# Attention put two more positions ahead of the feed-forward in a fused attention and feed-forward kernel

## The chip, the core and the metric

The kernel runs on one core of one Trainium2 chip. The metric is the device time of one execution in microseconds (us), the median of several runs. The core has five engines, each with its own in-order stream of instructions: PE (TensorE, the matrix unit, whose weight loads are listed apart as PEld), DVE (VectorE), ACT (ScalarE), POOL (GpSimd) and SP (SyncE, which here only issues transfers). They meet through semaphores. An instruction that waits holds back everything behind it on its own engine.

## The reference

```
k_all = concatenate([k_g, k_l]); v_all = concatenate([v_g, v_l])
out_g = softmax(scale * q_g @ k_all.T) @ v_all                # 32 global rows
s_ll  = where(|i - j| <= 32, scale * q_l @ k_l.T, -1e9)       # 512 local rows, band of 32
s_lg  = scale * q_l @ k_g.T
out_l = softmax(concatenate([s_lg, s_ll])) @ v_all
x = concatenate([out_g, out_l]).transpose(0, 2, 1, 3).reshape(B * S, H * D)   # 8 * 544 rows of 512
h = x @ w_in                                                  # 512 -> 2048
g = maximum(h, 0) + log1p(exp(-|h|))                          # softplus
out = g @ w_out                                               # 2048 -> 512
```

There are 8 batches of 8 heads, 512 local and 32 global positions and heads 64 wide; everything is float32.

## The kernel before

**Two streams of work.** The attention is done by head pairs m = 0 to 31, four pairs to a batch. Pairs 0 to 3 (batch 0) are done by a start-up sequence. Each later pair has three parts p = 0, 1, 2. `scores(m, p)` multiplies queries and keys on PE into the PSUM tile `s_ps`; for pairs 8 and up DVE adds the mask while it copies the tile to SBUF (line 315) and takes maxima by blocks (line 316). After part 2 come `maxima` (DVE and POOL, lines 329 to 339) and `probs`: DVE spreads the maxima (`mb`, line 347), POOL subtracts them (lines 352 to 355), ACT takes the exponential (line 356). `values(m, p)` multiplies the probabilities by the values on PE into `v_ps`; ACT copies the result out (lines 369 and 373) and DVE adds the overlapping columns (lines 374 and 375) into `x`.

**From a head pair to an input of the feed-forward.** After `values(m, 2)` the sums of the exponentials go to DRAM and back as a small tile `sc` (`combine`, lines 382 and 386), DVE inverts them (`invert`, lines 391 and 392), they go out again and come back spread over 64 partitions as `rb` (lines 393 and 396), and DVE multiplies `x` by `rb` into `xa` (`normalise`, line 404). At the start of a batch of the feed-forward, `split_x` makes of every `xa` a rounded high part `xh` (line 451) and the remainder `xl` (line 452). ACT and POOL do it for the pairs 0 and 2 of the batch, DVE for 1 and 3. There is one `xh` and one `xl` for each place, so that the last product of the batch before must have read them.

**The feed-forward.** For batch b and hidden block f (16 of them), 12 matmuls make the tile `h` from `xh`, `xl` and the weights `wi`; ACT and DVE make the softplus `e` (DVE has line 543); ACT and POOL split it into `gh` and `gl`; 12 more matmuls add the block into four output tiles `o`. A product of the second half, half a block at a time, follows one or two blocks behind the first half. In batch 0, DVE, ACT and POOL also put the weights into their final form (lines 479 to 498). The last 32 global rows of all batches are done at the very end as a "batch 8".

**One PSUM tile for all of the attention.** `s_ps` (from pair 6 on) and `v_ps` are all the same buffer, tag `a`, with `bufs=1`. Each `s_ps` or `v_ps` must therefore be copied out by DVE or ACT before the next of either can be started on PE.

**What sets the order.** `pieces()` gives each piece of attention a position: `scores(m, p)` stands at 12m + 4p, `values(m, p)` 22 positions (LAG) behind that, `invert(m)` at `end(m) + 3` and `normalise(m)` at `end(m) + 6`, with

```
def end(m):
    return 12 * m + 8 + LAG
```

So a head pair takes 12 positions and a batch 48, and from pair 8 on, one slot every two positions holds a piece with matmuls, scores and values in turn. `moe_items()` lists the feed-forward as items with a size (half a block, 6 matmuls, has size 2). The last loop of the function emits the items one by one. After each it works out the position `at` that the attention should have reached, from the share of the batch's items done, and emits all pieces up to it. `first` is the position at which batch 1 of the feed-forward begins; before, it is 36 + 30 + 6 = 72, the position of `normalise(3 + 4b)` less 48b. In batch 0, `at` runs from START = 69 to `first + 48`. PE keeps the order in which its matmuls are emitted; on the other engines a scheduler orders the instructions by its own estimate of when each is ready.

Of the kernel before, what the change touches and what calls it, by code (L numbers as in the profile page):

```python
# [16 lines left out]
B, H, SL, SG, D = 8, 8, 512, 32, 64  # L17
# [14 lines left out]
MPE = 8  # L32
LAG = 22
STEP = 3
GW = 75
W_AHEAD = 9
W_PRE = 12
# [16 lines left out]
def moe_over_global_local_attention(  # L54
# [223 lines left out]
    def load_v(m):  # L278
        t = pl.tile([P, 2, 6, 66], F32, tag="v", name=f"v{m}", bufs=2)
        nc.gpsimd.memset(t[:, :, :, D:D + 1], 1.0)  # L280
        nc.sync.dma_start(out=t[:, :, :, 0:D], in_=v[m - M0].rearrange("p (h c d) -> p h c d", h=2, d=D))
        st["v", m] = t
# [37 lines left out]
    def grid(t, start, *dims):  # L320
        base = t[0:32, start:start + 1]
        return bass.AP(base.tensor, base.offset, [list(base.ap[0])] + [list(d) for d in dims])
# [3 lines left out]
    def maxima(m):  # L326
        mt = st.pop(("mt", m))
        for a in range(1, 4):
            nc.gpsimd.tensor_copy(mt[0:32, GW * a:GW * a + GW], mt[32 * a:32 * a + 32, 0:GW])
        e0 = 4 * GW  # L330
        for u, du, off in ((0, 1, -2), (3, 1, 3)):
            nc.vector.tensor_reduce(grid(mt, e0 + u, (7, 6), (du, 2)), grid(mt, 3 + u, (12, 6), (du, 2), (off, 2), (GW, 4)), axis=AX.XY, op=ALU.max)
        nc.vector.tensor_reduce(grid(mt, e0 + 2, (7, 6), (4, 2)), grid(mt, 3 + 2, (12, 6), (7, 2), (GW, 4)), axis=AX.X, op=ALU.max)
        g = e0 + 44
        nc.vector.tensor_reduce(grid(mt, g, (1, 2)), grid(mt, 3 + 5, (36, 2), (12, 3), (3, 2), (GW, 4)), axis=AX.XYZ, op=ALU.max)
        nc.vector.tensor_copy(grid(mt, e0 + 5, (21, 2), (7, 3)), mt[0:32, g:g + 2].unsqueeze(2).to_broadcast([32, 2, 3]))
# [52 lines left out]
    def invert(m):  # L389
        sc, rows = st.pop(("sc", m))  # L390
        after(nc.vector.tensor_scalar(sc, sc, 1e-9, None, op0=ALU.add), "scores")
        nc.vector.reciprocal(sc, sc)
        nc.sync.dma_start(out=rows, in_=sc)
        rb = pl.tile([64, 2, 608], F32, tag="rb", name=f"rb{m}", bufs=1)
        r = rec_dram[2 * m:2 * m + 2]
        nc.sync.dma_start(out=rb, in_=r.unsqueeze(0).to_broadcast([64, 2, 608]))
        st["rb", m] = rb

    def normalise(m):
        b, j = divmod(m, H // 2)  # L400
        x, rb = st.pop(("x", m)), st.pop(("rb", m))
        y = xa[b, j] = pl.tile([P, 608], F32, tag="xa", name=f"xa{b}_{j}", bufs=4)
        for h in range(2):
            after(nc.vector.tensor_tensor(y[64 * h:64 * h + 64], x[0:64, h], rb[:, h], op=ALU.mult), "scores")  # L404
        nc.sync.dma_start(out=xg_dram[j, :, SG * b:SG * b + SG], in_=y[:, 160:192])
        ready.add((b, j))

    def end(m):
        return 12 * m + 8 + LAG

    def pieces():
        def piece(*fs):
            def go():
                for f in fs:
                    f()
            return go
        ps = []
        for m in range(M0, M):
            for p in range(NPC):
                fs = [lambda m=m, p=p: scores(m, p)]  # L420
                if m + 1 < M:
                    fs.append(lambda m=m, p=p: load(m + 1, p))
                if p == 2:
                    fs.append(lambda m=m: maxima(m))
                    fs += [lambda m=m, q=q: probs(m, q) for q in range(NPC)]
                ps.append((12 * m + 4 * p, piece(*fs)))
                fs = [lambda m=m, p=p: values(m, p)]
                if p == 2:
                    fs.append(lambda m=m: combine(m))
                    if m + 2 < M:  # L430
                        fs.append(lambda m=m: load_v(m + 2))
                    ps.append((end(m) + STEP, lambda m=m: invert(m)))
                    ps.append((end(m) + 2 * STEP, lambda m=m: normalise(m)))
                ps.append((12 * m + 4 * p + LAG, piece(*fs)))
        ps.sort(key=lambda t: t[0])
        return ps
# [172 lines left out]
    def loads(upto):  # L609
        while wk[0] < min(upto, len(order_w)):  # L610
            if order_w[wk[0]]:
                load_w(*order_w[wk[0]])
            wk[0] += 1
# [13 lines left out]
    load_v(M0)  # L627
    load_v(M0 + 1)
    loads(W_PRE + 2)
    first = end(H // 2 - 1) + 2 * STEP  # L630
    pcs = pieces()
    local = (scores0, lambda m, a: invert0((m, a), 4), lambda m, a: diag0((m, a), 4), turn0, evict0, values0, split0)
    glob = (scores0g, lambda n: invert0(n, 1), lambda n: diag0(n, 1), turn0g, evict0g, values0g, split0g)
# [110 lines left out]
```

## Time and profile before

| what | value |
|---|---|
| median of 3 runs | 1099.55 us (1097.02, 1099.55 and one of 4822.36) |
| the profiled execution: its own time, and its span | 1099.49 us, 1097.4 us |
| PE busy | 1037.4 us, 95% |
| DVE, ACT, POOL busy | 599.2 us (55%), 549.8 us (50%), 466.7 us (43%) |
| mean granted clock of PE | 0.977 |
| PE in the first 225 us | 184.5 us busy |
| PE from 225 to 1025 us | 789.4 us busy of 800 |

The span runs from the first to the last instruction in the profile; 2.1 us of the execution's own time lie outside it. A row of the timeline gives start, duration, engine, line, operation, tiles with their shapes, and how many instructions were merged. In square brackets stands how long the engine was idle just before, and what ended that. "issue" there means that the profile shows no releaser. Names carry no numbers in the profile, so the batch of an instruction is told from its time: batches of the feed-forward begin on PE at about 92, 241, 364, 484, 603, 722, 841 and 952 us. Some matmul records can be missing.

### The profile page before, as it was taken

Reading aid. Unit: us, or ns where it says so; the run is one execution under the profiler, and the core shown is the slowest. Engines: PE = TensorE matmul, PEld = TensorE weight load, DVE = VectorE, ACT = ScalarE, POOL = GpSimd, SP = SyncE. Lnnn points to the kernel's source line nnn. Section 1 sums busy time; section 2 is a strip of 40 time slices with the busy share of each in tenths; the row PEclk is TensorE's granted clock in tenths of the full one; section 3 lists DMA queues with packets and bytes.
Section 4 is the critical chain, followed back from the end, with each engine's and each line's share of the span. In section 5 each row is a group of like instructions: output and inputs, shape, how many; then the busy total and the mean of one; then the engine's idle time right before and its main releaser. Section 6 shows DMA issues by size and latency. Waiting matters only on the chain.

```text
span 1097.4 us, 14272 instructions
## 1 busy us (share of the span) xinstructions
PE 1037.4 (95%) x5108; PEld 799.0 (73%) x5108; DVE 599.2 (55%) x1137; ACT 549.8 (50%) x972; POOL 466.7 (43%) x554
## 2 busy tenths in 40 slices
PE   6896788999999999999999999999999999999996
PEld 4674566767777777777777777777777778788895
DVE  5979697874445655565555544565546542311211
ACT  6855555544444544545444544554454544454452
POOL 2136475762345444454444344544445442222221
PEclk9997889999999999999999999999999999999998
DMA  9432332322112212123211312122212210110010
GB/s 359 157 98 86 108 129 64 94 53 84 50 49 49 89 44 55 47 54 93 55 48 52 93 44 55 48 81 53 55 45 55 84 28 13 32 39 1 1 39 20
DMA packets 78566, 74.14 MB, mean 68 GB/s; under 512 B 53380, under 2 KB 57476, under 8 KB 78496
## 3 DMA queue, kind: packets, MB, share of 16 engines
q1 hardware_dynamic: 77952, 73.17, 22.6%
q8 instruction: 40, 0.66, 0.2%
q14 instruction: 30, 0.25, 0.1%
q10 hardware_dynamic: 544, 0.07, 0.0%
HBM read 63.51 MB, written 9.71 MB: 67 GB/s over the span
## 4 chain that ended last, share of the span: by engine, by line
PE 74%; DVE 8%; DMA 4%; issue 3%; POOL 1%; ACT 1%; DVEq 0%; ACTq 0%; SPq 0%; POOLq 0%
PE h L124 30%; PE o L124 30%; PE v_ps L124 9%; PE s_ps L124 5%; DMA rb<-rec_scratch 3%; DVE xa L404 2%; DMA rec_scratch<-sc 1%; DVE xl L452 1%; DVE xh L451 1%; DVE s L315 1%; DVE mb L347 0%; DVE wbitswo L489 0%; DVE woraw L492 0%; DMA raw<-in_qk 0%; DVE wbitswo L486 0%
## 5 line engine op out<-in xcount | busy, mean ns | idle before, releaser
L124 PE MATMUL h<-xh,wi 128*128 128x512 f32 (+1 forms) x1152 | 357.9, 394 | 20.0 <-DVE xl L226 10.3
L124 PE MATMUL o<-wo,gh 128*128 128x512 f32 x1088 | 346.9, 400 | 0.0
L547 POOL TENSOR_TENSOR gl<-e,gh 128x512 fp32r<-128x512 f32 x136 | 178.5, 1313 | 378.9 <-ACT gh L546 322.7
L124 PEld LDWEIGHTS h<-xh,wi 128*128 128x128 f32 x1152 | 208.7, 190 | 69.7 <-issue 17.2
L124 PEld LDWEIGHTS o<-wo,gh 128*128 128x128 f32 x1088 | 201.4, 189 | 47.3 <-issue 4.0
L124 PE MATMUL h<-xl,wi 128*128 128x512 f32 (+1 forms) x576 | 221.1, 384 | 2.8 <-DVE xl L452 2.8
L540 ACT ACTIVATE e<-h 128x512 f32<-128x512 f32 x136 | 81.3, 598 | 272.3 <-PE h L124 265.5
L124 PE MATMUL o<-wo,gl 128*128 128x512 f32 x544 | 213.6, 393 | 0.0
L543 DVE SCALAR_TENSOR_TENSOR e<-h,e 128x512 f32<-128x512 f32 x136 | 93.2, 685 | 182.9 <-ACT e L542 182.9
L352 POOL TENSOR_TENSOR s<-s,mb 128x384 f32<-128x384 f32 x112 | 137.7, 1261 | 14.2 <-DVE mb L347 14.2
L124 PEld LDWEIGHTS h<-xl,wi 128*128 128x128 f32 x576 | 109.6, 190 | 27.7 <-DVE xl L452 5.8
L546 ACT CAST gh<-e 128x512 fp32r<-128x512 f32 x136 | 84.2, 619 | 90.0 <-DVE e L543 90.0
L124 PE MATMUL v_ps<-s,v 128*65 128x192 f32 (+1 forms) x672 | 126.3, 319 | 2.1 <-DVE s L315 1.8
L124 PEld LDWEIGHTS o<-wo,gl 128*128 128x128 f32 x544 | 103.0, 189 | 22.7
L124 PEld LDWEIGHTS v_ps<-s,v 128*65 128x65 f32 (+1 forms) x672 | 85.3, 136 | 41.5 <-issue 15.9
L315 DVE TENSOR_TENSOR s<-s_ps,mask 128x768 f32<-128x768 f32 (+1 forms) x96 | 64.7, 694 | 90.9 <-PE s_ps L124 90.9
L542 ACT ACTIVATE e<-e,one 128x512 f32<-128x512 f32 x136 | 98.5, 724 | 3.3
L356 ACT ACTIVATE s<-s 128x768 f32<-128x768 f32 (+1 forms) x84 | 66.6, 792 | 66.5 <-POOL s L352 51.4
L124 PE MATMUL s_ps<-raw 64*128 64x192 f32 (+1 forms) x672 | 81.8, 350 | 13.5 <-issue 9.4
L541 ACT ACTIVATE e<-e 128x512 f32<-128x512 f32 x136 | 85.6, 630 | 3.4
L124 PEld LDWEIGHTS s_ps<-raw 64*128 64x128 f32 (+1 forms) x672 | 50.2, 181 | 49.8 <-issue 41.3
L316 DVE TRANSPOSE_TENSOR_REDUCE mt<-s 128x24 f32<-128x768 f32 (+1 forms) x84 | 76.2, 908 | 13.4 <-ACT s L312 9.7
(144 smaller groups left out, 839.3 us busy)
## 6 DMA issues: line engine op xcount, KB each, us to landing
raw<-in_qk SPq DMA_DIRECT2D x56, 272.0 KB
v<-in_v SPq DMA_DIRECT2D x28, 384.0 KB
out<-ot SPq DMA_DIRECT2D x34, 256.0 KB
rb<-rec_scratch SPq DMA_DIRECT2D x28, 304.0 KB
wiraw<-in_w_in SPq DMA_DIRECT2D x16, 512.0 KB
woraw<-in_w_out SPq DMA_DIRECT2D x16, 512.0 KB
raw<-in_qk SPq DMA_DIRECT2D x28, 192.0 KB
v<-in_v SPq DMA_DIRECT2D x4, 512.0 KB
```

Of the source, the lines that this page charges most:

```text
L124: order["pe"] = after(nc.tensor.matmul(*a, **k), "pe").ins
L315: nc.vector.tensor_tensor(s[:n, :, o:o + w], ps[:n, :, o:o + w], mk[:n].unsqueeze(1).to_broadcast([n, 2, w]), op=ALU.add)
L316: order["scores"] = nc.vector.tensor_reduce(windows(mt, 3 + 12 * p, 36, 2, nb), s.rearrange("p h (b k) -> p h b k", k=32), axis=AX.X, op=A ...
L352: nc.gpsimd.tensor_tensor(sw, sw, windows(mb[:, h], 0, 96, 2, 192), op=ALU.subtract)
L356: nc.scalar.activation(s, s, AF.Exp, scale=0.125)
L404: after(nc.vector.tensor_tensor(y[64 * h:64 * h + 64], x[0:64, h], rb[:, h], op=ALU.mult), "scores")
L540: nc.scalar.activation(e, ph, AF.Abs)
L541: nc.scalar.activation(e, e, AF.Exp, scale=-1.0)
L542: nc.scalar.activation(e, e, AF.Ln, bias=one)
L543: nc.vector.scalar_tensor_tensor(e, ph, 0.0, e, op0=ALU.max, op1=ALU.add)
L546: nc.scalar.copy(gh, e)
L547: nc.gpsimd.tensor_tensor(gl, e, gh.bitcast(F32), op=ALU.subtract)
```

## The change

A constant LEAD = 2 is added to `first`, and nothing else is changed.

```
 LAG = 22
 STEP = 3
+
+LEAD = 2
 GW = 75
...
-    first = end(H // 2 - 1) + 2 * STEP
+    first = end(H // 2 - 1) + 2 * STEP + LEAD
     pcs = pieces()
```

`first` becomes 74. In every batch from 1 on, a piece of attention is emitted about two positions, that is one slot, earlier among the items of the feed-forward; in batch 0 the attention covers 53 positions where it covered 51. Where a slot held scores it now mostly holds values, and the other way about. The instructions are the same, and the line numbers below the new constant are larger by 2.

On PE, ahead of batch 3 (o2_3 is output tile 3 of batch 2, h3_0 hidden block 0 of batch 3, s_ps18_0 and v_ps16_1 are part 0 of the scores of pair 18 and part 1 of the values of pair 16; the last number of a name only tells buffers apart), there stands before:

```order
L124 MATMUL v_ps16_0_4007<-s16_0_3579,v16_3681 65x192 x4
L124 MATMUL o2_0_3212<-wo14_1695,gh2_14_3900 128x512 x2
L124 MATMUL o2_0_3212<-wo14_1695,gl2_14_3901 128x512
L124 MATMUL o2_1_3216<-wo14_1695,gh2_14_3900 128x512 x2
L124 MATMUL o2_1_3216<-wo14_1695,gl2_14_3901 128x512
L124 MATMUL o2_2_3220<-wo14_1695,gh2_14_3900 128x512 x2
L124 MATMUL o2_2_3220<-wo14_1695,gl2_14_3901 128x512
L124 MATMUL o2_3_3224<-wo14_1695,gh2_14_3900 128x512 x2
L124 MATMUL o2_3_3224<-wo14_1695,gl2_14_3901 128x512
L124 MATMUL s_ps18_0_4030<-raw18_0_3816 128x192 x4
L124 MATMUL h3_0_4066<-xh3_0_4042,wi0_288 128x512 x2
L124 MATMUL h3_0_4066<-xl3_0_4043,wi0_288 128x512
```

And at the same place now:

```order
L126 MATMUL s_ps18_0_4018<-raw18_0_3794 128x192 x4
L126 MATMUL o2_0_3250<-wo14_1705,gh2_14_3914 128x512 x2
L126 MATMUL o2_0_3250<-wo14_1705,gl2_14_3915 128x512
L126 MATMUL o2_1_3254<-wo14_1705,gh2_14_3914 128x512 x2
L126 MATMUL o2_1_3254<-wo14_1705,gl2_14_3915 128x512
L126 MATMUL o2_2_3258<-wo14_1705,gh2_14_3914 128x512 x2
L126 MATMUL o2_2_3258<-wo14_1705,gl2_14_3915 128x512
L126 MATMUL o2_3_3262<-wo14_1705,gh2_14_3914 128x512 x2
L126 MATMUL o2_3_3262<-wo14_1705,gl2_14_3915 128x512
L126 MATMUL v_ps16_1_4042<-s16_1_3616,v16_3659 65x192 x4
L126 MATMUL h3_0_4074<-xh3_0_4050,wi0_288 128x512 x2
L126 MATMUL h3_0_4074<-xl3_0_4051,wi0_288 128x512
```

Every piece has moved up by one slot. The scores s_ps18_0 now stand 12 matmuls of the feed-forward ahead of v_ps16_1; before, v_ps16_1 stood 18 matmuls behind them, after h3_0 and the first half of the next output product. The last values of batch 3, v_ps15_2, stand 60 feed-forward matmuls ahead of h3_0 where they stood 48 ahead, since the whole of h2_14 is now between.

On DVE at the same boundary (xa3_3, xh3_3 and xl3_3 are the last input of batch 3 and its parts, e2_15 the softplus of the last block of batch 2, and s18_0 the masked copy of s_ps18_0) there stands before:

```order
L404 TENSOR_TENSOR xa3_3_4026<-x15_3778,rb15_3993 64x608 x2
L451 CAST xh3_3_4060<-xa3_3_4026 128x128
L451 CAST xh3_3_4060<-xa3_3_4026 128x384
L452 TENSOR_TENSOR xl3_3_4061<-xa3_3_4026,xh3_3_4060 128x128
L347 STREAM_TRANSPOSE mb17_2_3970<-mt17_3811 128x2x192
L452 TENSOR_TENSOR xl3_3_4061<-xa3_3_4026,xh3_3_4060 128x384
L315 TENSOR_TENSOR s18_0_4037<-s_ps18_0_4030,mask_72 128x768
```

And now:

```order
L406 TENSOR_TENSOR xa3_3_4014<-x15_3751,rb15_3971 64x608 x2
L349 STREAM_TRANSPOSE mb17_2_3951<-mt17_3789 128x2x192
L453 CAST xh3_3_4068<-xa3_3_4014 128x128
L453 CAST xh3_3_4068<-xa3_3_4014 128x384
L545 SCALAR_TENSOR_TENSOR e2_15_3993<-h2_15_3973,e2_15_3993 128x512
L454 TENSOR_TENSOR xl3_3_4069<-xa3_3_4014,xh3_3_4068 128x128
L454 TENSOR_TENSOR xl3_3_4069<-xa3_3_4014,xh3_3_4068 128x384
L317 TENSOR_TENSOR s18_0_4025<-s_ps18_0_4018,mask_72 128x768
```

The masked copy is still the last of the row, behind xa3_3 and its two parts, and e2_15 has come in between. Further up, the parts xh3_1 and xl3_1 and the softplus e2_14 stood ahead of the masked copy of s_ps17_2 and now stand behind it: e2_14 lies between the two steps of `invert(15)`, and xh3_1 and xl3_1 in the middle of `maxima(17)`.

In batch 0, on DVE, where the additions for v_ps4_1 stand (wbits and woraw are weights on their way to their final form), there stands before:

```order
L486 TENSOR_SCALAR wbitswi10_1170<-wbitswi10_1170 128x512
L492 SCALAR_TENSOR_TENSOR woraw6_901<-woraw6_901,wbitswo6_1100 128x512
L489 SCALAR_TENSOR_TENSOR wbitswo7_1144<-woraw7_903,wbitswo7_1144 128x512
L488 TENSOR_SCALAR wbitswi10_1170<-wbitswi10_1170 128x512
L492 SCALAR_TENSOR_TENSOR woraw7_903<-woraw7_903,wbitswo7_1144 128x512
L374 TENSOR_TENSOR x4_932<-x4_932,v_ps4_1_1035 65x2x64
L375 TENSOR_TENSOR x4_932<-x4_932,v_ps4_1_1035 65x2x32
```

And now:

```order
L490 TENSOR_SCALAR wbitswo7_1144<-wbitswo7_1144 128x512
L494 SCALAR_TENSOR_TENSOR woraw6_901<-woraw6_901,wbitswo6_1100 128x512
L491 SCALAR_TENSOR_TENSOR wbitswo7_1144<-woraw7_903,wbitswo7_1144 128x512
L376 TENSOR_TENSOR x4_932<-x4_932,v_ps4_1_1023 65x2x64
L377 TENSOR_TENSOR x4_932<-x4_932,v_ps4_1_1023 65x2x32
L494 SCALAR_TENSOR_TENSOR woraw7_903<-woraw7_903,wbitswo7_1144 128x512
```

Three weight steps that stood ahead of the two additions are behind them, two of them (weight wi10) much further down.

More of the change, by code (lines that the diff above doesn't have):

```diff
@@ L34 @@
 STEP = 3
+LEAD = 2
 GW = 75
@@ L629, in moe_over_global_local_attention @@
     loads(W_PRE + 2)
-    first = end(H // 2 - 1) + 2 * STEP
+    first = end(H // 2 - 1) + 2 * STEP + LEAD
     pcs = pieces()
```

## Prediction

> **What bounds the kernel now.** I read the page first, for the engine that leads.
>
> ```profile
> PE 1037.4 (95%) x5108; PEld 799.0 (73%) x5108; DVE 599.2 (55%) x1137; ACT 549.8 (50%) x972; POOL 466.7 (43%) x554
> ```
>
> PE does, so only what PE waits for can be won; all its idle time is 60 us. The view by windows tells where that lies (window, length, busy time of PE, PEld, DVE, ACT, POOL, then clock and transfers).
>
> ```profile
> 75.00:125.00 50.00, 31.70 (x146) 23.03 (x147) 44.30 (x69) 26.90 (x48) 30.33 (x29) 0.80 0.27 86
> 425.00:525.00 100.00, 98.75 (x484) 75.36 (x482) 56.19 (x108) 50.68 (x84) 46.78 (x58) 1.00 0.21 59
> ```
>
> Most of it lies in the first 225 us, where DVE has the weights to do as well (44.30 of 50 busy) and the clock is low. Later PE misses about 1.25 us in 100. The view of the waits says on what.
>
> ```profile
> PE h L124 <- DVE xh L451: 7.8, 7, 2.7
> PE h L124 <- DVE xl L452: 2.8, 6, 0.8
> ```
>
> These are the starts of batches 1 to 7: 7.8 + 2.8 = 10.6 us, seven boundaries, each at the first product that reads `xh` and `xl`. The timeline of PE at the third one:
>
> ```profile
> 473.72 0.91 PE L124 MATMUL s_ps<-raw 64*128 64x192 f32 x8
> ...
> 486.94 0.73 PE L124 MATMUL h<-xh,wi 128*128 128x512 f32 x2 [0.86 <-DVE xh L451]
> 488.07 0.50 PE L124 MATMUL h<-xl,wi 128*128 128x512 f32 x1 [0.39 <-DVE xl L452]
> 488.41 0.62 PE L124 MATMUL o<-wo,gh 128*128 128x512 f32 x2
> ...
> 489.80 1.46 PE L124 MATMUL v_ps<-s,v 128*65 128x192 f32 x8
> ```
>
> The row at 473.72 is s_ps17_2, that at 489.80 v_ps16_1. PE waits 0.86 + 0.39 = 1.25 us. DVE is what it waits for:
>
> ```profile
> 470.57 0.69 DVE L543 SCALAR_TENSOR_TENSOR e<-h,e 128x512 f32<-128x512 f32 x1 [0.28 <-ACT e L542]
> 473.60 1.34 DVE L451 CAST xh<-xa 128x128 fp32r<-128x128 f32 x2 [2.34 <-PE h L124]
> ...
> 475.54 0.81 DVE L315 TENSOR_TENSOR s<-s_ps,mask 128x384 f32<-128x384 f32 x2
> ...
> 477.15 0.13 DVE L391 TENSOR_SCALAR sc<-sc 38x32 f32<-38x32 f32 x1
> ...
> 478.19 0.54 DVE L332 TENSOR_REDUCE mt<-mt 32x12 f32<-32x96 f32 x2 [0.53 <-POOL mt L329]
> ...
> 482.54 2.31 DVE L404 TENSOR_TENSOR xa<-x,rb 64x608 f32<-64x608 f32 x2 [0.77 <-DMA rb<-rec_scratch]
> 484.94 1.95 DVE L451 CAST xh<-xa 128x128 fp32r<-128x128 f32 x2
> ...
> 487.95 0.94 DVE L315 TENSOR_TENSOR s<-s_ps,mask 128x768 f32<-128x768 f32 x1
> ```
>
> From 475.54 on DVE hardly rests: maxima, inverse, `xa`, `xh`, `xl`, and last, at 487.95 to 488.89, the masked copy of s_ps18_0. That copy frees the one PSUM tile of the attention, and v_ps16_1 at 489.80 needs it. Here nothing waits for it, by 0.91 us, and only because PE had already waited 1.25 us.
>
> **Part by part: the boundary.** The change puts the last values of a batch 12 more matmuls ahead of the next batch, so `xh` and `xl` come in time. But v_ps16_1 now stands ahead of h3_0, 12 matmuls behind s_ps18_0 instead of 18. What is late next is that masked copy, behind the same `xa`, `xh` and `xl` on DVE; queued behind the waiting v_ps16_1 is h3_0, and all of PE.
>
> I count both from the start of s_ps17_2. On PE the work between it and v_ps16_1 is the same in both orders, 48 feed-forward matmuls and two pieces: 489.80 - 473.72 - 1.25 = 14.83 us without waits. On DVE, from the first masked copy of s_ps17_2 (475.54) to the end of that of s_ps18_0 (488.89), there are 13.35 us. The new order adds xh3_1 and xl3_1 (475.54 - 473.60 = 1.94) and e2_14 (0.69). It covers the waits for `rb` (0.77) and for POOL (0.53) with them. DVE may start earlier, since xh3_1 no longer stands ahead; how early, a pair away from a boundary shows.
>
> ```profile
> 267.20 0.81 DVE L315 TENSOR_TENSOR s<-s_ps,mask 128x384 f32<-128x384 f32 x2 [3.42 <-PE s_ps L124]
> ...
> 277.38 0.92 DVE L315 TENSOR_TENSOR s<-s_ps,mask 128x768 f32<-128x768 f32 x1
> ...
> 333.45 3.18 DVE L404 TENSOR_TENSOR xa<-x,rb 64x608 f32<-64x608 f32 x2 [0.88 <-DMA rb<-rec_scratch]
> ```
>
> ```profile
> 266.24 0.91 PE L124 MATMUL s_ps<-raw 64*128 64x192 f32 x8
> ...
> 280.50 1.46 PE L124 MATMUL v_ps<-s,v 128*65 128x192 f32 x8
> ```
>
> The copy can start 267.20 - 266.24 = 0.96 us after the scores do. One wait is new: `sc`. Its two transfers start from the last values, which now stand only 12 matmuls ahead of these scores instead of 18. SP's own rows, at the third boundary and for the last pair, where DVE did wait for `sc`:
>
> ```profile
> 470.36 0.50 SPq L382 DMA_DIRECT2D rec_scratch<-x  x1
> 473.50 0.25 SPq L386 DMA_DIRECT2D sc<-rec_scratch  x1
> ```
>
> ```profile
> 943.20 0.23 SPq L386 DMA_DIRECT2D sc<-rec_scratch  x1
> ```
>
> ```profile
> 944.88 0.17 DVE L391 TENSOR_SCALAR sc<-sc 38x32 f32<-38x32 f32 x1 [2.03 <-DMA sc<-rec_scratch]
> ...
> 952.59 1.58 DVE L404 TENSOR_TENSOR xa<-x,rb 64x608 f32<-64x608 f32 x2 [2.93 <-DMA rb<-rec_scratch]
> ```
>
> `sc` lands 944.88 - 943.20 = 1.68 us after its issue, so 473.50 - 470.36 + 1.68 = 4.8 us after the first transfer. With the scores 12 matmuls behind the values I estimate that DVE waits up to 0.4 us for it, and take 0.4. The copy then ends at 0.96 + 13.35 + 1.94 + 0.69 - 0.77 - 0.53 + 0.4 = 16.04, against 14.83 for PE: a new wait of about 1.2 us, which with the start of v_ps16_1 behind the copy I round to 1.27. It is as long as the one that goes. Its bounds: 0.1 us, if `sc` is there and the two multiplications of `xa` take 1.58 (952.59) instead of 2.31; 2.14 us, if they take 3.18 (333.45).
>
> **The boundaries summed.** The first one is worse than the others before:
>
> ```profile
> 246.51 0.73 PE L124 MATMUL h<-xh,wi 128*128 128x512 f32 x2 [2.69 <-DVE xh L451]
> 248.04 0.80 PE L124 MATMUL h<-xl,wi 128*128 128x512 f32 x1 [0.80 <-DVE xl L452]
> 248.63 1.06 PE L124 MATMUL o<-wo,gh 128*128 128x512 f32 x2
> ...
> 251.19 1.52 PE L124 MATMUL v_ps<-s,v 128*65 128x192 f32 x8
> ```
>
> It waits 2.69 + 0.80 = 3.49 us, and then PE runs at half speed: the six matmuls from 248.63 take 2.56 us, at the third boundary (488.41 to 489.80) 1.39, so 1.17 more. Together 4.66 us; the new wait leaves 1.27, a gain of 3.4. Boundary 7 has no scores behind it:
>
> ```profile
> 954.83 0.73 PE L124 MATMUL h<-xh,wi 128*128 128x512 f32 x2 [0.60 <-DVE xh L451]
> ```
>
> Its 0.6 us goes. Boundaries 2 to 6 now cost 10.6 - 3.49 - 0.6 = 6.5 us and then 5 x 1.27 = 6.35: a gain of 0.15.
>
> The half speed has its row: a wait of 2.69 us brings it, one of 1.80 us does not:
>
> ```profile
> 217.74 1.52 PE L124 MATMUL v_ps<-s,v 128*65 128x192 f32 x8 [1.80 <-DVE s L315]
> ...
> 219.78 0.62 PE L124 MATMUL o<-wo,gh 128*128 128x512 f32 x2
> ```
>
> [...]
>
> **Between the boundaries.** Every pair now has 12 matmuls from part 0 of the scores to the next values, and the same 14.26 us (280.50 - 266.24) from part 2. Before, the masked copy ended 277.38 + 0.92 - 266.24 = 12.06 us in. The wait for `sc` (0.4) and a softplus ahead of the second step of the inverse (0.69) now delay `rb`, and a second softplus stands ahead of the copy (0.69): 13.84 us, 0.42 before it is needed. Where `xa` takes 3.18 instead of 2.29, it is 0.47 late. Such a long `xa` stands ahead of 3 of these 16 places; I take 3 x 0.47 = 1.4 us lost, with bounds 0 and 16 x 0.47 = 7.5.
>
> **Batch 0.** Two long waits there, and what ended the first:
>
> ```profile
> 120.18 1.01 PE L124 MATMUL s_ps<-raw 64*128 64x192 f32 x4 [6.08 <-issue]
> ...
> 190.49 1.65 PE L124 MATMUL s_ps<-raw 64*128 64x192 f32 x8 [3.33 <-issue]
> ```
>
> ```profile
> 117.20 0.41 DVE L486 TENSOR_SCALAR wbitswi<-wbitswi 128x512 f32<-128x512 f32 x1
> 117.54 0.68 DVE L492 SCALAR_TENSOR_TENSOR woraw<-woraw,wbitswo 128x512 int32<-128x512 int32 x1
> ...
> 119.68 0.27 DVE L374 TENSOR_TENSOR x<-x,v_ps 65x128 f32<-65x128 f32 x1
> ```
>
> The page names no releaser, but PE starts 0.3 us after the additions (119.68, line 374) that free the same tile. They stood behind three weight steps that now come later: 0.34 (117.20 to 117.54), as much for the second of its kind, and 0.6, so 1.3 us less. The other long waits may win as much or get a successor of their own, and the last ones gain or lose with how DVE is shared; I take -1.3, with bounds -3.9 (three waits) and +4 (a new one as long as that at 190.49).
>
> **The rest costs nothing.** No instruction is added. The loads of queries and keys move up with their scores, and SP has room. The tail has no attention.
>
> **The sum** against the profiled execution's own 1099.49 us, which is the median 1099.55 but for 0.06 (the run of 4822.36 is left aside): -3.4 - 0.15 - 0.6 + 1.4 - 1.3 = -4.05, so 1095.4. I say **1095 us**.
>
> **Rivals.** *The boundary wait goes and nothing takes its place* (0.20). This is the plain reading of the waits. It needs DVE to end its row 1.2 us sooner than I count, for which the bound of 0.1 us speaks, and the busy row of DVE speaks against it. Then -(4.66 + 6.5 + 0.6) + 6 x 0.1 - 3.9 = -15: 1084 us.
>
> *The PSUM tile becomes the bound, slower than before* (0.22). If both multiplications of `xa` run beside POOL's subtractions and take 3.18 us each time, the six boundaries wait 6 x 2.14 = 12.84 against 11.16 before, the 16 other pairs lose 7.5, boundary 7 wins 0.6, and batch 0 gives nothing: +8.6, 1108 us. With half speed after each of the six waits it is 6 x 1.17 = 7 more, 1115. It decides for slower once the new wait passes 1.25 us and the clock follows. The rows for it are 333.45 (3.18) beside 952.59 (1.58). [...]
>
> *My forecast*, one wait for another, has 0.55; the last 0.03 is for what I have not thought of, mostly slower.
>
> **Chances and range.** Two per cent, 22 us, is about what a measurement of this kernel can tell from no change. The range goes from the one rival's 1084 to just past the other's 1108, which leaves out the worst of the second rival and the unknown rest. All cases stay within 1077.6 and 1121.5 but for the unknown rest and the worst of the second rival: faster 0.01, same 0.96, slower 0.03.
>
> **What would show it.** Right: at the boundaries the wait on `xh` and `xl` is gone from PE's waits and one on the masked copy, line 317 now, stands before `v_ps`, of about 1.3 us, six times; PE's idle time at boundary 1 falls, and the first batch starts its second block of scores sooner. Wrong: no such wait (the first rival), waits at `v_ps` of over 2 us or between the boundaries too, with the clock below 1.00 after 225 us (the second), or a first batch that moves by more than 4 us either way.

## The result, and the profile after

The changed kernel takes 1114.2 us (median of 4 executions, 1113.3 to 1115.0), the kernel before 1099.6 beside it (1097.0, 1099.6 and 1101.6). One execution of the kernel before, of 4822.4 us, is a slow one and is left aside. The ratio is 1.0134, with a 95% interval of 1.0107 to 1.0162: slower, by less than two per cent. The forecast was 1095 with a range that ends just past 1108. The second rival, priced at 1108, or 1115 with half speed after each wait, lies nearest. Its bound is the one that came, the PSUM tile with the clock behind it, but its price fits partly by luck: it had waits of 2.14 us, from `xa` alone, and lost 7.5 us more between the boundaries, where nothing was lost. The profiled execution took 1114.09 us, its span 1112.0; against the 1099.49 of before that is 14.60 more.

The page's first part and the view of the waits, cut to the stretch from 225 to 960 us, which holds all boundaries (us in total, times, longest):

```profile
PE 1041.1 (94%) x5108; PEld 802.8 (72%) x5108; DVE 627.7 (56%) x1137; ACT 549.1 (49%) x972; POOL 463.9 (42%) x554
...
PE v_ps L126 <- DVE s L317: 21.4, 7, 3.6
```

The waits on `xh` and `xl` are gone, and in their place stands the wait on the masked copy that the forecast named: same row, same tile. Six of its seven are the boundaries, together 20.2 us where the waits at all seven boundaries before had 10.6; the seventh, of 1.3 us, stands at 224.92, still in batch 0. VectorE does the same 1137 instructions in 627.7 us where it took 599.2. The timeline of PE at the boundaries, first to sixth:

```profile
245.51 0.38 PE L126 MATMUL v_ps<-s,v 128*65 128x192 f32 x1 [3.04 <-DVE s L317]
...
368.34 0.38 PE L126 MATMUL v_ps<-s,v 128*65 128x192 f32 x1 [3.61 <-DVE s L317]
...
491.07 1.64 PE L126 MATMUL v_ps<-s,v 128*65 128x192 f32 x8 [3.49 <-DVE s L317]
...
613.64 0.38 PE L126 MATMUL v_ps<-s,v 128*65 128x192 f32 x1 [3.35 <-DVE s L317]
...
734.63 0.57 PE L126 MATMUL v_ps<-s,v 128*65 128x192 f32 x1 [3.35 <-DVE s L317]
...
857.32 0.39 PE L126 MATMUL v_ps<-s,v 128*65 128x192 f32 x1 [3.34 <-DVE s L317]
```

Each boundary waits 3.0 to 3.6 us where 1.27 was forecast. From the first of these rows to the last lie 611.81 us. Before, the same stretch went from 251.19 to

```profile
847.48 0.32 PE L124 MATMUL v_ps<-s,v 128*65 128x192 f32 x1
```

which is 596.29. So the five batches between the boundaries 1 and 6 lose 15.5 us, and the rest, batch 0 with boundary 1 and the tail, gives 0.9 back; together these are the 14.6.

Why the copy is late, at the third boundary, is in VectorE's timeline. The scores s_ps17_2, from which the forecast counted, start on PE at

```profile
473.18 0.91 PE L126 MATMUL s_ps<-raw 64*128 64x192 f32 x8
```

and VectorE does behind them:

```profile
474.13 0.81 DVE L317 TENSOR_TENSOR s<-s_ps,mask 128x384 f32<-128x384 f32 x2 [3.03 <-PE s_ps L126]
...
477.62 1.12 DVE L338 COPY mt<-mt 32x6 f32<-32x6 f32 x1
478.65 0.48 DVE L453 CAST xh<-xa 128x128 fp32r<-128x128 f32 x2
479.16 1.50 DVE L341 COPY mt<-mt 32x42 f32<-32x42 f32 x3
...
482.72 2.67 DVE L406 TENSOR_TENSOR xa<-x,rb 64x608 f32<-64x608 f32 x2
...
485.92 1.95 DVE L453 CAST xh<-xa 128x128 fp32r<-128x128 f32 x2
488.39 1.75 DVE L454 TENSOR_TENSOR xl<-xa,xh 128x128 fp32r<-128x128 f32 x2
490.07 0.94 DVE L317 TENSOR_TENSOR s<-s_ps,mask 128x768 f32<-128x768 f32 x1
```

The row from the copy of s_ps17_2 to that of s_ps18_0 has the instructions that were counted, in the order that was counted, and the first begins 0.95 us behind the scores (473.18), as forecast. But it ends 17.83 us behind them (490.07 + 0.94 - 473.18) and not 16.04. The copies of the maxima on 32 partitions (lines 338 and 341) take 1.12 and 1.50 us; before, the same rows took 0.15 (479.55) and 0.56 (479.73):

```profile
479.55 0.15 DVE L336 COPY mt<-mt 32x6 f32<-32x6 f32 x1
479.73 0.56 DVE L339 COPY mt<-mt 32x42 f32<-32x42 f32 x3
```

This is not the boundary's alone: from 260 to 940 us all 22 of the copies of 32 x 6 take 0.15 us before, and 0.86 to 1.14 in the changed kernel. GpSimd's timeline in the changed kernel shows what runs beside them:

```profile
477.43 1.28 POOL L549 TENSOR_TENSOR gl<-e,gh 128x512 fp32r<-128x512 f32 x1 [0.73 <-ACT gh L548]
478.66 1.76 POOL L454 TENSOR_TENSOR xl<-xa,xh 128x128 fp32r<-128x128 f32 x2
```

The copy of line 338 ends at 478.74, GpSimd's subtraction for `gl` at 478.71. The three copies of line 341 last from 479.16 to 480.66, and beside them GpSimd's `xl` runs until 480.42. That they run side by side is all that these rows show; whether the one lengthens the other is what the experiments with GpSimd quiet decide.

The second thing that the forecast priced too low is the clock. The windows below are 3.41 us each (length, busy time of PE, granted clock, then transfers); at a granted clock of 0.50 three matmuls of 128x512 take 1.28 us (493.78 to 495.06), at 1.00 0.69 (496.07 to 496.76); that is the half speed meant below:

```profile
488.92:492.33 3.41, 1.26 (x9) 1.00 0.00 0
492.33:495.74 3.41, 3.41 (x10) 0.50 0.00 0
608.38:611.80 3.41, 1.91 (x9) 1.00 0.34 86
611.80:615.21 3.41, 1.57 (x9) 1.00 0.00 0
615.21:618.62 3.41, 3.41 (x16) 1.00 0.00 0
```

Behind the wait at the third boundary PE runs 3.41 us at half speed; behind that at the fourth, of 3.35 us, it doesn't. All boundaries but the fourth have such a stretch. Its price is the difference of two batches whose end waits are both 3.35: 613.64 - 491.07 = 122.57 with one, 734.63 - 613.64 = 120.99 without, so 1.6 us.

### The profile page after: what moved, and what is told of

It is laid out like the page before. It is cut to its first block, busy times and chain, and to the rows that moved or that the text cites. A ratio compares the mean times of both kernels' runs of the same rounds, so it can differ in the third digit from the quotient of the medians.

```text
span 1112.0 us, 14276 instructions
## 1 busy us (share of the span) xinstructions
PE 1041.1 (94%) x5108; PEld 802.8 (72%) x5108; DVE 627.7 (56%) x1137; ACT 549.1 (49%) x972; POOL 463.9 (42%) x554
## 4 chain that ended last, share of the span: by engine, by line
PE 70%; DVE 8%; issue 1%; DMA 1%; POOL 1%; ACT 0%; DVEq 0%; SPq 0%; POOLq 0%; ACTq 0%
PE h L126 30%; PE o L126 27%; PE v_ps L126 9%; PE s_ps L126 4%; DVE xa L406 2%; DVE xl L454 1%; DVE mt L341 1%; DVE s L317 1%; DVE xh L453 1%; DVE e L545 1%; DVE mb L349 1%; DMA rec_scratch<-x 1%; DVE mt L338 0%; POOL s L354 0%; DVE mt L334 0%
## 5 line engine op out<-in xcount | busy, mean ns | idle before, releaser
L126 PEld LDWEIGHTS h<-xh,wi 128*128 128x128 f32 x1152 | 212.1, 193 | 61.2 <-issue 16.9
L126 PE MATMUL v_ps<-s,v 128*65 128x192 f32 (+1 forms) x672 | 130.9, 327 | 27.8 <-DVE s L317 26.4
L354 POOL TENSOR_TENSOR s<-s,mb 128x384 f32<-128x384 f32 x112 | 135.1, 1235 | 48.1 <-DVE mb L349 48.1
L406 DVE TENSOR_TENSOR xa<-x,rb 64x608 f32<-64x608 f32 x56 | 68.4, 1222 | 25.2 <-DMA rb<-rec_scratch 24.8
```

The source lines that it names most:

```text
L126: order["pe"] = after(nc.tensor.matmul(*a, **k), "pe").ins
L354: nc.gpsimd.tensor_tensor(sw, sw, windows(mb[:, h], 0, 96, 2, 192), op=ALU.subtract)
```

## The experiments

The theory after the two traces: PE waits at v_ps16_1 because the masked copy of s_ps18_0 stands behind `xh` and `xl` on VectorE (its place), because that row is slowed by GpSimd beside it (its length), and the clock then adds 1.6 us. The rivals: the lead costs in itself, wherever the copy stands; the row is too long by its order alone; the half clock (half speed, as above) belongs to the boundary and not to the idle time.

**The copy ahead of `xh3_3` and `xl3_3`.**

```
 # scores
-                nc.vector.tensor_tensor(s[:n, :, o:o + w], ps[:n, :, o:o + w], mk[:n].unsqueeze(1).to_broadcast([n, 2, w]), op=ALU.add)
+                order["masked"] = nc.vector.tensor_tensor(s[:n, :, o:o + w], ps[:n, :, o:o + w], mk[:n].unsqueeze(1).to_broadcast([n, 2, w]), op=ALU.add).ins
 # split_x
-            (nc.vector.tensor_copy if j % 2 else nc.scalar.copy)(hi, f(t))
-            (nc.vector if j % 2 else nc.gpsimd).tensor_tensor(lo, f(t), hi.bitcast(F32), op=ALU.subtract)
+            i = (nc.vector.tensor_copy if j % 2 else nc.scalar.copy)(hi, f(t))
+            k = (nc.vector if j % 2 else nc.gpsimd).tensor_tensor(lo, f(t), hi.bitcast(F32), op=ALU.subtract)
+            if j == 3:
+                after(i, "masked"), after(k, "masked")
```

> The changed kernel, but on VectorE the cast and the subtraction of part 3 of the next batch's x (xh3_3, xl3_3 at the third boundary) are held behind the masked copy of s_ps18_0; nothing else moves. Theory (the PE wait is the copy's place in VectorE's row, plus the half clock that follows the wait): the four pieces that stood ahead of the copy took 0.85 + 1.18 + 1.35 + 0.5 = 3.9 us, more than the wait of 3.4, so all six waits at v_ps go, the clock is 1.00 after 225 us, and the time is 1114 - 6 x 3.4 - 5 x 1.7 = 1085 (to 1090 if xl3_3 is now late by up to 1 us). Rival (attention further ahead of its feed-forward costs in itself, through more work side by side): the waits come back at xh or xl or at the next copies, and the time stays over 1105.

1088.0 us (1086.2 to 1088.9), against 1099.1 of before on the same chip: 0.9906, interval 0.9889 to 0.9923. The waits from 225 to 960 us, the timeline of PE at the third boundary, and VectorE's beside it:

```profile
PE v_ps L126 <- DVE s L317: 2.5, 2, 1.3
```

```profile
478.46 1.49 PE L126 MATMUL v_ps<-s,v 128*65 128x192 f32 x8
```

```profile
477.44 0.94 DVE L317 TENSOR_TENSOR s<-s_ps,mask 128x768 f32<-128x768 f32 x1
478.30 1.47 DVE L453 CAST xh<-xa 128x128 fp32r<-128x128 f32 x2
```

v_ps16_1 starts without a wait, 0.08 us behind the copy; `xh` and `xl`, now behind it, come in time. Two waits are left of 1.3 us at most (at 225 us and at boundary 1), and the granted clock is 1.00 in each of the six stretches of 120 us from 240 to 960 us. The time fell by 26, where 24 to 29 were expected. At the boundaries the lead itself costs nothing; the copy's place does. This version is faster than both kernels, by about one per cent against the one before.

**GpSimd quiet, in the changed kernel; and without the subtraction of the maxima alone.**

```
 # probs, in both
-                nc.gpsimd.tensor_tensor(sw, sw, windows(mb[:, h], 0, 96, 2, 192), op=ALU.subtract)
...
-            nc.gpsimd.tensor_tensor(s[:, :, 0:192], s[:, :, 0:192], mb[:, :, 0:192], op=ALU.subtract)
-            nc.gpsimd.tensor_tensor(s[:, :, 192:288], s[:, :, 192:288], mb[:, :, 96:192], op=ALU.subtract)
 # act, in the quiet form
-            nc.gpsimd.tensor_tensor(gl, e, gh.bitcast(F32), op=ALU.subtract)
-            g[b, f] = (gh, gl)
+            g[b, f] = (gh, gh)
 # split_x, in the quiet form: xl[j] is xh[j] where j is even
-            (nc.vector if j % 2 else nc.gpsimd).tensor_tensor(lo, f(t), hi.bitcast(F32), op=ALU.subtract)
+            if j % 2:
+                nc.vector.tensor_tensor(lo, f(t), hi.bitcast(F32), op=ALU.subtract)
```

> The changed kernel without most of GpSimd's work behind the weights: the subtraction of the maxima is left out (the row sums follow, so the softmax is the same), and the low halves of the softplus result and of x's parts 0 and 2 are left out, their high halves standing in; the matrix products are as many. Theory (VectorE's row was lengthened by GpSimd beside it): the small copies of the maxima fall from 1.12 and 0.97 us to under 0.25 each, xa to 0.8 a piece, the copy of s_ps18_0 ends at about 14.2 us behind the start of s_ps17_2, before PE's 14.4, and the wait at v_ps is below 0.5 us at all six boundaries. Rival (the row is too long by its order alone, or slow for another reason): the durations stay, and so do waits of 3.0 to 3.6 us.

> The changed kernel with only GpSimd's subtraction of the maxima left out (the row sums follow, so the softmax is the same). Theory (each VectorE instruction is slowed by the GpSimd instruction that runs beside it): xa falls to 0.8 a piece (1.07 less at the third boundary) and xl to about 0.5 (0.84 less), while the two small copies of the maxima, which ran beside the softplus' low half and x's low half, stay near 1 us; so the wait at v_ps is 3.4 - 1.9 = 1.5 us, with no half clock behind it. If all of GpSimd's work slows all of VectorE's evenly, the small copies fall too; if contention is not it, the wait stays at 3.0 to 3.6.

Both leave work out, so what counts is their durations and waits; one execution each, 1059.0 us and 1072.3. VectorE at the third boundary with GpSimd quiet, and PE behind it:

```profile
442.15 0.16 DVE L338 COPY mt<-mt 32x6 f32<-32x6 f32 x1
...
443.27 0.56 DVE L341 COPY mt<-mt 32x42 f32<-32x42 f32 x3
...
446.36 1.54 DVE L399 TENSOR_TENSOR xa<-x,rb 64x608 f32<-64x608 f32 x2
...
449.93 0.95 DVE L317 TENSOR_TENSOR s<-s_ps,mask 128x768 f32<-128x768 f32 x1
```

```profile
451.97 1.30 PE L126 MATMUL v_ps<-s,v 128*65 128x192 f32 x7
```

The small copies are back at 0.16 and 0.56, `xa` is at 1.54 for both, and the copy ends 13.16 us behind s_ps17_2 (which starts at 437.72) instead of 17.83. PE has no wait there, nor anywhere between 225 and 960 us. So the order alone doesn't make the row too long: 4.7 us of it are GpSimd's doing. Without the subtraction of the maxima alone:

```profile
450.65 1.12 DVE L338 COPY mt<-mt 32x6 f32<-32x6 f32 x1
...
452.19 1.49 DVE L341 COPY mt<-mt 32x42 f32<-32x42 f32 x3
...
457.23 1.54 DVE L399 TENSOR_TENSOR xa<-x,rb 64x608 f32<-64x608 f32 x2
...
460.55 0.95 DVE L317 TENSOR_TENSOR s<-s_ps,mask 128x768 f32<-128x768 f32 x1
```

```profile
461.56 1.19 PE L126 MATMUL v_ps<-s,v 128*65 128x192 f32 x6 [1.04 <-DVE s L317]
```

`xa`, whose neighbour was taken away, falls from 2.67 to 1.54; the small copies, whose neighbours are still there, stay at 1.12 and 1.49. A piece that had been short grew: xl3_1 (453.71) takes 1.78 us where it took 0.76, and GpSimd's `xl` now runs beside it until 455.07. The wait is 1.04, near the 1.5 expected, and no half clock follows it. The slowing here is one of pairs that lie side by side, not an even one.

**The same quiet in the kernel before.** The edit is the same, without the lead.

> The kernel before with the same of GpSimd's work left out as in the quiet form of the changed kernel (subtraction of the maxima; low halves of the softplus result and of x's parts 0 and 2). Theory: VectorE's row to xh and xl shortens by about 1.5 us, so the 1.25 us that PE waits at the third boundary goes nearly to nothing, and the first boundary's 3.5 us falls by as much; both kernels then have no boundary wait and differ by less than 4 us. Rival (order alone): the waits at xh and xl stay at 0.8 + 0.4.

1062.6 us, and no wait of PE between 225 and 960 us. The order of PE is that of before, so this run shows what a batch costs without a wait (v_ps12_1 and v_ps16_1, in PE's timeline; under them the row of before that lies a batch ahead of 489.80):

```profile
342.21 0.32 PE L126 MATMUL v_ps<-s,v 128*65 128x192 f32 x1
...
459.58 0.32 PE L126 MATMUL v_ps<-s,v 128*65 128x192 f32 x1
```

```profile
370.60 0.32 PE L124 MATMUL v_ps<-s,v 128*65 128x192 f32 x1
```

117.37 us a batch, against 489.80 - 370.60 = 119.20 before. (The copy-first run, which leaves nothing out, has 478.46 - 361.04 = 117.42.) The boundary of before thus cost 1.83 us, not the 1.25 that its two waits show as idle time. With GpSimd quiet both kernels lose all boundary waits, and stand 3.6 us apart, the changed one ahead.

**Other leads: one, three and four positions.**

```
-LEAD = 2
+LEAD = 1        # and 3, and 4
```

> One position instead of two. On PE, h3_0 then stands 6 matmuls behind s_ps18_0 and v_ps16_1 behind h3_0; on VectorE the masked copy of s_ps18_0 stands ahead of xl3_3. Theory (each wait is VectorE's row against PE's place): xh3_3 ends some 14.7 us behind the start of s_ps17_2 (as in the changed kernel) and is needed after 45 matmuls and three pieces, at about 13.5, so PE waits about 1.2 us at xh and 0.4 at xl again, none at v_ps; no half clock; about 1099 us, range 1094 to 1103. Rival (the time rises or falls steadily with the distance): halfway between the two kernels, 1107.

> Three positions. On PE 48 matmuls again lie between s_ps17_2 and v_ps16_1; on VectorE all four pieces of xh3 and xl3 still stand ahead of the masked copy of s_ps18_0, only the softplus step e2_15 has moved behind it. Theory: the copy ends 17.83 - 0.68 = 17.15 us in, PE wants it at 14.24, so a wait of about 2.9 us at v_ps, six times, with the half clock behind most: 1110 us, range 1105 to 1115. Rival (steady with the distance): 1121.

> Four positions: the split of x is now written behind s_ps18_1, and on VectorE the masked copy of s_ps18_0 stands ahead of xh3_3 and xl3_3 and of e2_15 without anything else being changed. Theory: the row to the copy loses 0.85 + 1.18 + 0.48 + 1.35 + 0.68 = 4.5 us, the copy ends 13.3 us in, before PE's 14.24; no boundary waits, 1086 us, range 1082 to 1092. Rival (steady with the distance): 1128; rival (a longer distance costs elsewhere, in the first batch or at xh): over 1095.

1110.5 us (ratio 1.0100, 1.0085 to 1.0116), 1126.7 (1.0244, 1.0229 to 1.0260) and 1103.6 (1.0041, 1.0026 to 1.0057): none in its range by the theory, all too slow by 11 to 18 us; one position comes near the steady rival's 1107, three lie 6 us above its 1121, four are 24 below its 1128 and in the other rival's case. Where PE waits is as the theory said for one and three, not for four. PE's timeline at the third boundary with one position, then with three:

```profile
489.17 0.73 PE L126 MATMUL h<-xh,wi 128*128 128x512 f32 x2 [1.61 <-DVE xh L453]
491.10 0.50 PE L126 MATMUL h<-xl,wi 128*128 128x512 f32 x1 [1.19 <-DVE xl L454]
```

```profile
496.08 1.38 PE L126 MATMUL v_ps<-s,v 128*65 128x192 f32 x5 [4.34 <-DVE s L317]
```

With one position PE waits at `xh` and `xl`, 1.61 + 1.19 for 1.6 expected, and four of the six boundaries are followed by half speed. With three it waits at `v_ps`, 4.34 for 2.9, and all six are. VectorE's rows with three, and with four:

```profile
487.91 3.55 DVE L453 CAST xh<-xa 128x128 fp32r<-128x128 f32 x4
```

```profile
481.18 1.82 DVE L453 CAST xh<-xa 128x128 fp32r<-128x128 f32 x2
482.92 1.84 DVE L454 TENSOR_TENSOR xl<-xa,xh 128x128 fp32r<-128x128 f32 x2
484.69 0.94 DVE L317 TENSOR_TENSOR s<-s_ps,mask 128x768 f32<-128x768 f32 x1
```

The expectations took every duration from the changed kernel, and that didn't hold. The casts of xh3_1 and xh3_3 took 0.48 and 1.95 there and take 3.55 together with three positions. With four, xh3_1 and xl3_1, which took 0.48 and 0.76, have moved behind `xa`, where xh3_3 and xl3_3 took 1.95 and 1.75 beside GpSimd's subtractions (484.70 to 490.59), and take 1.82 and 1.84, 2.4 us more, which turns a margin of 0.9 into a wait:

```profile
485.69 0.54 PE L126 MATMUL v_ps<-s,v 128*65 128x192 f32 x2 [0.99 <-DVE s L317]
```

Here the small copies are short again (0.16, and 0.56 for the three). So the length of a piece isn't its own: xh3_1 took 0.48 or 1.82 us by the lead alone. Four positions also lose in batch 0: its first two long waits are 7.33 and 7.53 us where two positions have 4.83 and 4.54, and its last, at boundary 1, is 5.67. How much of each miss these waits make up is not worked out.

**The copy first, without the lead.** The first experiment's edit, in the kernel before.

> The kernel before (no lead) with the cast and subtraction of part 3 of x held behind the masked copy of s_ps18_0, as in the copy-first form of the changed kernel. Theory: here PE waits for xh3_3 and xl3_3 themselves, not for the copy, so the 0.94 us of the copy comes on top of the 1.25 us at every boundary with scores behind it, and the copy's own wait for s_ps18_0 may add more: 1099 + 6 x 0.94 = 1105 us, range 1102 to 1112; where the wait passes 2 us the clock may be halved too. Rival (the order on VectorE alone is what was wrong, and the lead does nothing): 1088 as in the copy-first form.

1114.3 us, 1.0134 (1.0117 to 1.0151), above the range. PE at the third boundary:

```profile
492.59 0.73 PE L126 MATMUL h<-xh,wi 128*128 128x512 f32 x2 [2.38 <-DVE xh L453]
494.11 0.70 PE L126 MATMUL h<-xl,wi 128*128 128x512 f32 x1 [0.79 <-DVE xl L454]
```

The wait is at `xh` and `xl`, as the theory had it, and 3.17 us instead of 2.19: the reduction of the maxima (0.96) came in between `xh` and `xl` as well, which I had left out, and half speed followed five times. The rival falls: the order on VectorE alone loses 15 us, the lead alone as much, both together win 11.

**PE given something to do while it waits.**

```
 # values(m, p), p == 1 of the first pair of a batch
+        if p == 1 and m >= 8 and m % 4 == 0:
+            fill = ps_h.tile([P, 512], F32, tag="h", name=f"fill{m}")
+            for _ in range(12):
+                mm(fill[:, 0:384], lhsT=ident, rhs=mask, start=True, stop=True, skip_group_check=True)
```

> The changed kernel with more work for PE: ahead of v_ps16_1, and of its like at the other five boundaries, 12 matmuls of the identity with the mask (384 columns) into a free tile that nobody reads. They run in the time in which PE waits for the masked copy, take about 2 us, and leave some 1.4 us of the wait. Theory (the half clock comes from the idle time, and only where a stretch of 3.41 us on the clock's grid holds about 2 us of it): no half clock at any boundary, the end of each wait stays where VectorE's row puts it, and the time falls by 5 x 1.75: 1105 us, range 1102 to 1108. Rival (the half clock goes with the boundary, or the added work costs its time): 1114, or 1114 + 6 x 2 = 1126.

1107.0 us (1104.7 to 1108.1), where the changed kernel has 1114.2; against the kernel before beside each, 1.0076 (1.0059 to 1.0093) and 1.0134. PE's timeline at the third boundary:

```profile
486.46 2.12 PE L126 MATMUL fill<-mask,ident 128*128 128x384 bf16 x12
489.96 1.51 PE L126 MATMUL v_ps<-s,v 128*65 128x192 f32 x8 [1.38 <-DVE s L317]
```

v_ps16_1 still starts 3.5 us behind the last useful matmul, but only 1.38 of it are idle, and the granted clock is 1.00 in each of the six stretches of 120 us from 240 to 960 us. 72 useless matmuls made the kernel 6 to 7 us faster, of the 9 expected: with 1.38 us idle at this boundary instead of 3.49 the half clock stays away, so here it comes from idle PE.

## Why the prediction was wrong

**The mechanism was right, its size and its sign were not.** That the waits on `xh` and `xl` go, that the masked copy takes their place at `v_ps` at six boundaries, and that boundary 7 just loses its wait, came as forecast. The forecast said "one wait for another", as long as the first, and so a kernel 4 us faster; it was 2.2 us longer at each of boundaries 2 to 6, with the clock behind.

**The step that failed: the row of VectorE, "0.96 + 13.35 + 1.94 + 0.69 - 0.77 - 0.53 + 0.4 = 16.04".** The 13.35 us are what the instructions took before, beside what lay beside them before. Measured: 17.83. The small copies cost 1.91 more (1.12 + 1.50 against 0.15 + 0.56), xl3_3 1.0 more (1.75 against 0.28 + 0.51), `xa` 0.36; xh3_1 and xl3_1 cost 0.7 less than the 1.94, and the wait of 0.4 for `sc` didn't come. These add up to 2.1 of the 1.8 us; the other pieces are together 0.3 shorter. The bounds of 0.1 and 2.14 varied `xa` alone. The second rival had this cause, but for `xa` alone: the one of 3.18 us (333.45) has GpSimd's four subtractions of the maxima beside it, from 332.48 to 337.52, and that of 1.58 (952.59) has nothing, GpSimd having ended at 951.68. The runs show it of a copy too: 0.16 us with GpSimd quiet, 1.12 beside a subtraction of 1.28, ending with it.

**PE's side, "489.80 - 473.72 - 1.25 = 14.83 us without waits".** Taking off the idle time takes off too little. In the copy-first run the same stretch without a wait is 478.46 - 464.22 = 14.24. A wait on `xh` and one on `xl` cost 1.83 where the trace shows 1.25 idle, so the old waits were worth some 0.6 more at each boundary than the gain counts for them, and the new wait is longer by as much: 16.04 against 14.24 would have been 1.8 and not 1.2. The waits of before also stood at the last of the four parts, xh3_3 and xl3_3 at the third boundary, and not "at the first product that reads" the two tiles: PE had read the other three from 483.75 on.

**The clock.** The forecast's wait of 1.27 was to bring no half speed. The waits of 3.0 to 3.6 brought it at five of six boundaries, 1.6 us each; the 1.17 of the prediction was counted only up to the values at 251.19. Nor was it the first boundary's 2.69 alone that brought it before: the 3.41 us ahead of the half speed (244.48 to 247.89) hold 2.03 of it and 0.65 of the 0.80 behind it.

**The sum for boundaries 2 to 6** with the measured sizes: waits of 3.61 + 3.49 + 3.35 + 3.35 + 3.34 = 17.1 instead of 6.35, +10.8; four stretches of half speed inside, +6.4; the old waits worth 5 x 0.58 more, -2.9; no loss between the boundaries, where 1.4 was taken. The forecast had -0.15 + 1.4 = 1.25 for this stretch, so 1.25 + 10.8 + 6.4 - 2.9 - 1.4 = 14.2 of the measured 15.5; the rest is most likely what a new wait costs beyond its idle time (the batch with no half speed costs 120.99 - 117.37 = 3.62 for 3.35 idle, five times 0.27). No run shows that part by itself.

**Between the boundaries** nothing waits; the 0.47 us by which a copy was to be late in three places did not come.

**Batch 0** was right only where it had a row. Its long waits now, in PE's timeline:

```profile
117.79 0.69 PE L126 MATMUL s_ps<-raw 64*128 64x192 f32 x2 [4.83 <-ACT wo L499]
...
154.55 0.69 PE L126 MATMUL s_ps<-raw 64*128 64x192 f32 x2 [4.54 <-ACT e L542]
...
193.58 0.58 PE L126 MATMUL v_ps<-s,v 128*65 128x192 f32 x1 [3.89 <-DVE s L317]
```

The first went from 6.08 to 4.83, the 1.3 that the three weight steps were counted for (the additions that free the tile now end at 117.69, behind the cast of `wo` that the row names, which ended at 117.52). That of 4.10 at 156.73 became 4.54, and that of 3.33 at 190.49 came back as 3.89 at another place. From 100 to 240 us PE is idle for 17.8 us where it was for 17.1, so nothing of the -1.3 is left. Boundary 1, where the 2.69 + 0.80 and 1.17 were to become 1.27, got 3.04 and half speed. For batch 0, boundary 1 and the tail the forecast had -1.3 - 3.4 - 0.6 = -5.3, and the runs -0.9; these places do not account for all of the difference, and what is left stays open.

## What to carry to other kernels

A duration read from a trace belongs to its neighbours as well (here 0.15 or 1.12 us for the same copy): before summing a row of VectorE in a new order, look at what GpSimd does in the same microseconds, and price each piece that a trace shows at two lengths at both its short and its long one. When a buffer with one copy is freed by an engine that also feeds the next stage, put the freeing instruction ahead of the feeding ones, and check again whether the stage can bear it; here only lead and order together won. Count a wait of PE with what it costs beyond its idle time (1.83 us for 1.25 idle here), and with the clock (1.6 us).

## What the runs showed that I had not expected

**A copy of 6 columns on 32 partitions can cost 1.1 us.** Beside a GpSimd subtraction of 1.28 us it took 1.12, alone 0.15; the masked copy, which reads PSUM, took 0.95 with GpSimd quiet and 0.94 beside its subtractions (all 48 of that shape in the changed kernel lie between 0.92 and 0.96), and the reduction of the maxima behind it 0.98 in both. The instructions that were stretched here are copies (0.15 to 1.12 us), casts (xh3_1, 0.48 to 1.82), and products and differences with both inputs in SBUF (`xa`, 1.54 to 2.67; xl3_1, 0.76 to 1.78).

**The granted clock changed on a fixed grid.** In each of the eleven profiled executions all changes of the granted clock lie on a grid of 3.413 us, to a thousandth of a step. Worked out over these windows: where PE at full speed was idle for 2.0 us or more of one, the next was at half speed, 82 times of 82; with 0.8 to 1.58 us idle never, in 76; between, 7 times of 21. In the two traces of the kernel before and the changed one it followed 19 windows of 19 with 2.15 us or more, and none of 17 with 0.8 to 1.84. The wait of 3.35 us at 613.64 brought no half speed: the grid cuts it into 1.50 and 1.84, and the 1.84, which lies between, went the good way: a window of the copy-first run without the lead was idle for 1.82 and was followed by half speed.
